# Shared channel rows of an mLSTM mixer computed as fp32 products in the two column halves of TensorE, results written to freed tiles, and a new task order

## Chip, cores and metric

One core of a Trainium2 chip. The metric is the device time in microseconds (us) of one execution, taken as the median of the runs. TensorE's two clock levels are 1.2 and 2.4 GHz; a granted clock of 1.00 in a row is 2.4 GHz, 0.50 is 1.2 GHz.

## The reference, cut to what matters

```python
for t in range(S):                      # S = 768, B = 4, H = 8, D = 40
    ...                                 # gates with a running maximum
    C = f_stab[:, :, None, None] * C + i_stab[:, :, None, None] * np.einsum('bhd,bhe->bhde', vt, kt)
    n = f_stab[:, :, None] * n + i_stab[:, :, None] * kt
    ...
    y[:, :, t] = o * h_tilde / denom
# x: y as (B, S, 320)
theta = x @ w_theta
zr = x * cos(theta); zi = x * sin(theta)
u = x + einsum('ts,bsd->btd', w_tok_r, zr) + einsum('ts,bsd->btd', w_tok_i, zi)
return u + maximum(u @ w_ch, 0.0)       # the channel product
```

All inputs are float32 in value; the weights of the mixer come to the chip as 64-bit words and are rounded there.

## The kernel before, in words

The kernel has three parts. The attention works in 24 units (6 chunks of 128 tokens by 4 batches): small fp32 products of 64-wide tiles (score L442, state L463, inter L482, intra L491). The mixer works in 12 pieces (a chunk by a pair of batches): five transposes (L538), the angle product (L554, L560), sine and cosine, and then five token products (L605, `mix`) of 12 matmuls each, whose result VectorE adds into `acc` (L630). `acc` holds u transposed: 10 tiles of 128 channel rows by 768 tokens, five for each pair of batches. Tile 2 of each five is shared: its upper 64 rows are the last 64 channels of the pair's first batch, its lower 64 rows the first 64 of the second batch.

The last part is the channel product, `channel()`. Each number that TensorE is to multiply with nearly full precision is split into a rounded high part and the rest (type fp32r, `_hi` and `_lo` tasks, and `uhi`, `ulo` at L669 and L670 for `acc`), and a product is made of three matmuls: high by high, low by high, high by low (`prods`, L680). Tiles 0, 1, 3 and 4 need two full blocks of 128 rows (L688) and one half block of 64 rows, which two tiles do at once in the two row halves of the array (L698). The shared tile 2 needs five full blocks, since its two batches' weights stand beside zeros in one 128-column operand: 5 blocks by 3 matmuls by 2 halves of the tokens are 30 matmuls for each pair of batches, at L688. VectorE adds the clipped result to `acc` in place (`relu`, L713), and SyncE sends the rows out (`out`, L715). The weights lie in two tiles of the pool `w`, with zeros between them (L641).

All work is a list of tasks; `ORDER`, a table written out by hand, gives the order of the tasks and each one's engine (T TensorE, V VectorE, A ScalarE, G GpSimd, D a DMA on SyncE's queue). Every engine runs its instructions in that order. `FILL` puts dummy matmuls of `ones` (L247) ahead of some TensorE tasks. Tiles come from small pools in the order of the tasks: four PSUM tiles `two`, three `tok`, three `z`, three `w`, two `raw`. A task that takes a buffer waits until the last user of that buffer is done.

Names used below: `tok4` is the load of the keys and values of attention unit 4 (L422), `w10` a block of token weights (L373), `st4` the state product of unit 4 (L463), `mix01` the token product of chunk 0, row tile 1, and `zl` the low part of a rotated mixer tile (L592).

Of the kernel before, what the change touches and what calls it, by code (L numbers as in the profile page):

```python
# [17 lines left out]
DM = H * D  # L18
# [15 lines left out]
WCOLS = 1792  # L34
# [6 lines left out]
4G 5T 6T 7T 8T 0D 14V 284V 85V 1D 21A 18A 12G 3G 30G 11V 13V 15D 43D 16D 55D 25V 27V 19V 28V 81V 29V 104D 47D 26V 44A  # L41
31V 82V 2D 32V 35A 83V 38V 37V 33A 17A 123D 39T 24A 56A 84V 280V 103D 34V 36V 42A 100A 99A 40A 282V 23V 86V 48A 109A
283V 102V 285V 101A 281V 49V 98A 41A 20A 110T 50V 90A 105T 22A 107T 57V 111V 51V 106A 128A 58V 52A 286V 108V 122D 59V
124T 125A 126T 53A 91V 127V 129T 212T 192D 130V 60A 292G 265G 61V 213A 74D 197A 131T 67D 132T 211D 54V 133V 139G 87V
134V 92V 135V 88A 75A 261G 62V 136V 291V 137V 112T 114V 113T 140V 138G 66A 193T 64A 63A 120G 93G 115V 116V 194A 117V
118V 121V 119V 198T 216A 76V 89V 94T 141T 77V 95A 97A 142A 143V 68A 96A 69V 78V 293T 263A 144A 65A 145T 70V 388D 191D
146T 296A 294A 295A 79A 147A 158T 71V 159T 195T 148V 160A 161V 199V 196V 72A 149A 162A 150A 200T 80G 297D 210D 45D
201T 163A 208G 202V 217T 214T 73V 151A 218A 203V 152V 219T 165V 204V 155V 166A 264V 273D 368D 167G 215V 369D 299D 221V
153A 220T 205V 209V 266D 222V 164A 154G 262A 168V 301T 223V 156V 169V 157V 179T 170V 298A 46A 224V 206V 302A 300D 320D
225V 207V 274A 305G 175T 180T 176T 325G 226V 229T 227V 228V 178A 232A 230A 275V 276V 181V 177V 327G 182A 171T 231V  # L50
172T 277V 173V 307G 303T 306T 304V 308V 376G 278A 267A 233T 234T 279G 374G 309T 235A 174V 321T 311V 236V 440D 310T
322A 319D 237A 326T 312V 313A 238A 268V 187T 314V 315V 317V 318V 316G 328V 188T 189V 183T 239A 323T 190A 329T 240V
243V 324V 184T 241A 287A 375T 331V 337G 242V 338V 244A 377V 330T 186A 185V 332V 245G 441A 378T 389D 386G 289A 333A
370T 380V 334V 269V 288V 387V 335V 252T 336G 253V 254V 371A 436A 438A 249T 390T 339T 270V 396G 391A 340A 251V 250V
456D 342V 341V 442V 255T 372T 373V 256V 343T 457D 611D 366D 437A 271A 367A 593A 344T 257A 462G 464G 394G 443V 395T
435A 345A 272V 379T 246T 397V 346V 381V 347A 444V 290V 349A 247V 398T 400V 348A 382V 392T 393V 258T 353V 439G 406G
350V 458T 248A 407V 260V 259V 463T 447D 354A 399T 465V 383V 546D 401V 478T 351A 459A 460T 352V 479A 402A 384V 403V
385V 525D 404V 477D 466T 355G 405G 445A 448A 468V 461V 356T 474G 449V 357V 408T 409A 358T 410V 412T 413T 450V 475V
411V 446G 359V 482G 533G 553G 454D 476D 455A 414A 467T 469V 415V 470A 594A 471V 595V 480T 483T 621G 484G 416A 418A
472V 417A 604D 523D 485V 481V 362T 473G 486T 363V 488V 494G 487T 547T 489V 495V 490A 422G 491V 423A 419V 420A 548A  # L60
360T 527T 364T 605A 750A 528A 424V 421V 492V 451V 365V 614D 425T 493G 452A 427T 606V 496T 607V 361V 426V 608V 453G
429T 526D 613D 545D 597D 524A 497A 598A 592A 619A 609A 531G 596G 753G 551G 498V 500T 501T 502A 428V 430V 529T 532T
599V 499V 610G 549T 530V 503V 431T 534V 504A 535T 505A 550V 600V 432V 506A 552T 543G 554V 536T 544V 537V 538V 555T
557V 507G 510V 508A 563V 433T 511A 615T 509V 911D 512G 564V 556T 434V 912A 617T 558V 634D 620T 601V 513T 616A 539A
540V 559A 560V 612A 602A 561V 541V 622V 562G 542G 514V 517T 618V 565T 633D 518V 566A 567V 568V 515T 623T 839D 683D
680D 688G 603G 569T 681A 639A 710G 570T 516V 625V 641V 571A 751A 631G 913V 632V 914V 572V 573V 575A 640T 624T 626V
642V 519T 574A 754D 643T 637T 520V 645V 682D 579V 635T 690G 651G 521T 652V 636A 580V 684T 576V 704T 638V 577A 685A
703D 522V 644T 689T 581G 686T 768D 702D 771D 705A 752A 627A 578V 628V 646V 749A 755A 647A 629V 691V 648V 586T 687V
692T 630G 649V 650G 708G 700G 587V 693T 653T 694V 654A 695V 756V 696V 701V 582T 772T 655V 773A 657T 658T 659A 656V
697V 583V 757V 706T 758V 660V 709T 661A 588T 698V 707V 711V 776G 712T 778G 699G 720G 589V 770D 663A 714V 713T 774T  # L70
721V 791D 662A 667V 777T 779V 715V 775V 759A 668A 590T 716A 717V 718V 664G 719G 584T 780T 790D 840D 669V 591V 585V
# [18 lines left out]
1112T 1113T 1114T 1140T 1117V 1125D 1141V 1143T 1115V 1116D 1118D 1142D 1144V 1145D  # L90
"""
FILL = """
39:6 107:2 110:6 113:3 124:2 126:2 200:1 201:1 214:2 217:2 219:2
"""


# [62 lines left out]
def mlstm_mixer(ctx: ExitStack, tc: tile.TileContext, gates, qk, tok, og, wtok, wth, wch, table_d, out):  # L159
# [472 lines left out]

    def channel():
        wc = [Tile(w_k, F32R), Tile(w_k, F32R)]
        wcv = lambda a: wc[a].t
        up = {}

        def zeros(e):
# [27 lines left out]
        for pr in range(2):  # L666
# [6 lines left out]
            if pr == 0:  # L673
                for jj in range(5):
                    pm[jj, 1] = pm[jj, 0]
# [157 lines left out]
```

## Time and profile before

| what | value |
|---|---|
| median of 3 runs | 296.83 us (296.46 to 298.31) |
| the profiled execution, its own time | 298.13 us |
| its span, first to last instruction | 296.3 us |
| mean granted TensorE clock | 0.987 |

The profile is of one execution, and durations are read from it; 1.8 us of its time lie outside the span. PE is TensorE's matmuls, PEld its weight loads, DVE VectorE, ACT ScalarE, POOL GpSimd, SP SyncE. The ends of matmuls are modelled, so that a pace is read from one start to the next, or from a piece of the chain of waits, and not from the mean of one.

### The profile page before, as it was taken

The numbers are of one execution on the slowest core, as the hardware profiler recorded it, in microseconds if no ns is written. First come the engines' busy times: TensorE is split into PE (matmuls) and PEld (weight loads), VectorE is DVE, ScalarE is ACT, GpSimd is POOL, SyncE is SP. The second block draws the span as 40 slices with busy tenths as digits, with TensorE's granted clock in tenths as the row PEclk, the third lists the DMA queues.
The fourth block names the chain that finished last, engine by engine and source line by source line (L and its number), as shares of the span: only waits on it lengthen the run. The fifth ranks groups of instructions, "written<-read, shape, count | busy, mean of one in ns | idle before, by whom it ended". The sixth has DMA issues, their size and how long they took to land.

```text
span 296.3 us, 10261 instructions
## 1 busy us (share of the span) xinstructions
PE 283.7 (96%) x4467; PEld 256.2 (86%) x4467; DVE 240.5 (81%) x449; ACT 180.8 (61%) x332; POOL 118.8 (40%) x125
## 2 busy tenths in 40 slices
PE   8598897999999999999999999999999999999995
PEld 3366677899899998999999999999999999999885
DVE  6869898699899998988998888888899697684342
ACT  6989998596876887858445493586377456120000
POOL 1003221635156474453517655333153529355000
PEclk9879999999999999999999999999999999999999
DMA  6967766545355551844417714525002000002334
GB/s 229 328 193 244 239 186 197 195 140 173 109 165 187 172 171 45 269 163 153 110 50 217 257 47 119 158 94 161 8 3 88 2 0 0 0 2 79 135 147 171
DMA packets 13484, 40.08 MB, mean 135 GB/s; under 512 B 1536, under 2 KB 3328, under 8 KB 13440
## 3 DMA queue, kind: packets, MB, share of 16 engines
q1 hardware_dynamic: 13440, 39.43, 41.7%
q8 instruction: 35, 0.57, 0.8%
q14 instruction: 9, 0.07, 0.1%
HBM read 35.49 MB, written 3.93 MB: 133 GB/s over the span
## 4 chain that ended last, share of the span: by engine, by line
PE 86%; DMA 5%; ACT 5%; DVE 1%; SPq 1%; issue 1%; POOL 0%; DVEq 0%
PE two L605 42%; PE two L688 10%; PE two L554 7%; PE two L442 4%; PE two L482 4%; PE two L491 4%; PE two L560 3%; PE two L463 3%; DMA tok<-in_tok 3%; PE two L430 3%; DMA raw<-in_wth 2%; PE two L538 2%; PE two L432 2%; ACT tok L451 2%; PE two L247 1%; PE two L698 1%
## 5 line engine op out<-in xcount | busy, mean ns | idle before, releaser
L605 PE MATMUL two<-w,z 128*128 128x384 f32 x720 | 135.5, 341 | 0.2 <-DVE hv L503 0.2
L605 PEld LDWEIGHTS two<-w,z 128*128 128x128 f32 x720 | 123.8, 188 | 1.8 <-issue 0.4
L630 DVE TENSOR_TENSOR acc<-two,acc 128x768 f32<-128x768 f32 x50 | 46.9, 951 | 12.3 <-PE two L605 11.9
L519 POOL TENSOR_TENSOR X<-hv,sg 128x320 f32<-128x320 f32 x18 | 16.1, 903 | 45.3 <-DVE sg L516 45.3
L688 PE MATMUL two<-u,w 128*128 128x384 f32 x156 | 28.7, 340 | 0.1
L688 PEld LDWEIGHTS two<-u,w 128*128 128x128 f32 x156 | 26.9, 188 | 1.4 <-issue 1.0
L368 POOL TENSOR_TENSOR w<-val,w 128x768 fp32r<-128x768 f32 (+2 forms) x11 | 20.1, 1832 | 12.9 <-ACT w L367 10.7
L473 POOL TENSOR_TENSOR C<-C,wane 128x164 f32<-128x164 f32 x34 | 17.2, 515 | 19.3 <-PE two L482 18.1
L554 PE MATMUL two<-wth,xs 128*128 128x320 f32 x144 | 23.7, 312 | 0.8 <-ACT wane L351 0.8
L713 DVE SCALAR_TENSOR_TENSOR acc<-two,acc 128x384 f32<-128x384 f32 (+1 forms) x15 | 9.7, 687 | 17.2 <-PE two L698 10.4
L554 PEld LDWEIGHTS two<-wth,xs 128*128 128x128 f32 x144 | 21.6, 188 | 1.4 <-ACT wane L351 1.0
L434 ACT ACTIVATE E<-two 128x512 f32<-128x512 f32 x24 | 14.1, 597 | 12.6 <-PE two L432 12.4
L564 ACT ACTIVATE r<-two 128x640 f32<-128x640 f32 (+1 forms) x13 | 8.6, 663 | 17.7 <-PE two L560 17.7
L445 DVE TENSOR_TENSOR E<-two,E 128x512 f32<-128x512 f32 x24 | 16.3, 682 | 3.2 <-PE two L442 2.1
L453 POOL TENSOR_TENSOR tok<-tok,fadeT 128x320 f32<-128x320 f32 x16 | 13.0, 815 | 12.2 <-DMA tok<-in_tok 12.1
L463 PE MATMUL two<-tok 64*40 64x41 f32 x768 | 13.2, 204 | 4.9 <-ACT tok L451 3.2
L592 POOL TENSOR_TENSOR z<-ab,z 128x640 fp32r<-128x640 f32 x8 | 14.2, 1779 | 8.5 <-ACT z L590 6.8
L670 POOL TENSOR_TENSOR u<-acc,u 128x768 fp32r<-128x768 f32 x7 | 14.4, 2068 | 8.0 <-DVE u L669 8.0
L463 PEld LDWEIGHTS two<-tok 64*40 64x40 f32 x768 | 10.6, 116 | 7.9 <-ACT tok L451 3.8
L482 PEld LDWEIGHTS two<-C,qk 40*64 40x64 f32 x768 | 13.8, 134 | 4.0 <-issue 2.1
L442 PEld LDWEIGHTS two<-qk 40*64 40x64 f32 x768 | 13.8, 138 | 4.1 <-issue 3.1
L442 PE MATMUL two<-qk 40*64 40x64 f32 x768 | 16.8, 227 | 0.0
(123 smaller groups left out, 534.2 us busy)
## 6 DMA issues: line engine op xcount, KB each, us to landing
qk<-in_qk SPq DMA_DIRECT2D x24, 448.0 KB, 4.9
raw<-in_wtok SPq DMA_DIRECT2D x12, 768.0 KB, 4.5
tok<-in_tok SPq DMA_DIRECT2D x24, 324.0 KB, 4.0
sg<-in_og SPq DMA_DIRECT2D x12, 320.0 KB, 4.2
out<-acc SPq DMA_DIRECT2D x5, 384.0 KB, 2.4
out<-acc SPq DMA_DIRECT2D x10, 192.0 KB, 2.3
raw<-in_wth SPq DMA_DIRECT2D x2, 480.0 KB, 7.0
raw<-in_wch SPq DMA_DIRECT2D x1, 640.0 KB, 3.8
```

The lines of the kernel that those rows point to most:

```text
L368: add(name + "_lo", "GV", lambda e: ENG[e].tensor_sub(lo(), o(), hi().bitcast(F32)), [val, *rest], step)
L442: nc.tensor.matmul(u.sc.t[half[x ^ f], f, k * L:(k + 1) * L], q4(1)[dims[f], k, s], q4(0)[dims[f], k, s], start=True, stop=True)
L445: add(f"wg{n}", "V", lambda e: nc.vector.tensor_mul(u.E.t, u.sc.t[:, :, :4 * L], u.E.t), [u.sc, u.E], n)
L463: nc.tensor.matmul(u.st.t[dims[f], x, k * E1:(k + 1) * E1], kt()[r, h], vt()[r, h], start=True, stop=True)
L473: add(f"cw{x}{n}", "GV", lambda e: ENG[e].tensor_mul(C[b][1 - x], C[b][x], f), (), n + 0.2)
L482: nc.tensor.matmul(u.it.t[half[x], f, k * E1:(k + 1) * E1], q4(0)[dims[f], k, s], C[b][x][dims[f], k], start=True, stop=True)
L519: add(f"X{n}", "VG", lambda e: ENG[e].tensor_mul(u.X.t[:, b % 2 * DM:(b % 2 + 1) * DM].rearrange("p (h d) -> p h d", d=D), u.hv.t[:, :, :D ...
L554: nc.tensor.matmul(th.t[:, b, :DM], xs.t[:, x, k], wt5[:, y, k], start=(i == l == 0), stop=False)
L605: nc.tensor.matmul(pm.t[:, t, :TH], Z[cc, pr].t[:, x, s, j * P:(j + 1) * P], wv(cc, y, s, t), start=(s == 1 and x == y == 0 and cc == mine ...
L630: add(f"ga{q}{j}", "V", lambda e, j=j, pm=pm, av=av: nc.vector.tensor_add(av, pm.t[:, :, :TH], av), [pm], n + 2.6 + 0.3 * j, swap="acc")
L670: add(f"ulo{pr}{k}", "VG", lambda e, pr=pr, k=k: ENG[e].tensor_sub(up[pr, k][:, 1], acc[:, 5 * pr + k], up[pr, k][:, 0].bitcast(F32)), (), ...
L688: nc.tensor.matmul(pv(jj, t), wcv(x)[:, col:col + P], up[pr, k][:, y, cols], start=(i == l == 0), stop=(jj == 2 and i == 4 and l == 2))
```

## The change

The shared tile 2 is no longer made of split operands. A small fp32 tile `wx` holds its weights whole: six blocks of 128 rows by 64 columns, three for each of the two batches (the two half blocks are filled up with zeros). The products are plain float32, with `acc` itself as the moving operand; the first batch's go to PSUM partitions 0 to 63 and the second's to 64 to 127, that is to the two column halves of the array, in turn (`shared`, L712 of the changed kernel). `uhi` and `ulo` stay, for the other tiles. Since `acc` must stay whole until then, `relu` writes into a tile of the pool `z` that the mixer has left, and `out` sends from there. The second pair of batches is no longer cut by halves of the tokens, but for its shared tile. The weights lie close together in `w`, so the four zero fills are gone; `wx` needs two smaller ones and seven copies. `_layout` sends the channel weights in the same form as the angle weights. `ORDER` is new for all tasks, and `FILL` has two dummy matmuls more.

```diff
-WCOLS = 1792
 ORDER = """
-4G 5T 6T 7T 8T 0D 14V 284V 85V 1D 21A 18A 12G 3G 30G 11V 13V 15D 43D 16D 55D 25V 27V 19V 28V 81V 29V 104D 47D 26V 44A
+4G 5T 6T 7T 8T 0D 30V 3V 1D 85G 11G 12G 14G 25V 43D 15D 27V 16D 55D 104D 2D 47D 17A 28V 123D 26V 103D 29V 122D 284G
...
 FILL = """
-39:6 107:2 110:6 113:3 124:2 126:2 200:1 201:1 214:2 217:2 219:2
+39:6 94:1 105:1 110:6 124:3 131:2 141:3 198:1 200:2 201:1 214:2 219:3
 """
...
+            up["wx"] = upool.tile([P, 6, L], F32, name="wx")
...
+        def zeros(e):
+            nc.scalar.activation(wx()[L:, 2], ident[L:, :L], AF.Copy, scale=0.0)
+            nc.scalar.activation(wx()[:L, 5], ident[:L, :L], AF.Copy, scale=0.0)
+
+        def whole0(e):
+            v = vals[0].t
+            COPY[e](wx()[:, 0:2], v[:, :2 * DM].rearrange("p (k n) -> p k n", k=2)[:, :, 4 * L:])
+            COPY[e](wx()[:L, 3], v[L:, 0:L])
+            COPY[e](wx()[L:, 3], v[:L, DM:DM + L])
+            COPY[e](wx()[:L, 4], v[L:, DM:DM + L])
...
-            fulls = {0: [(0, 0), (1, 704)], 1: [(0, P), (1, 704 + P)], 3: [(3, 384 + 64), (4, 1088 + 64)],
-                     4: [(3, 384 + 64 + P), (4, 1088 + 64 + P)], 2: [(0, 256), (1, 960), (2, 1664), (3, 320), (4, 1024)]}
...
+            def shared(t, pr=pr, pm=pm):
+                cols = slice(t * TH, (t + 1) * TH)
+                for i in range(3):
+                    for g in range(2):
+                        k = 2 if i == 2 else 3 * g + i
+                        nc.tensor.matmul(pm[2].t[L * g:L * g + L, t, :TH], wx()[:, 3 * g + i], acc[:, 5 * pr + k, cols],
+                                         start=(i == 0), stop=(i == 2))
+
+            def leave(jj, o, t0, t1, late, pr=pr, pm=pm):
+                ov = lambda: o.t.rearrange("p a s n -> p (a s n)")[:, (jj // 3) * S + t0 * TH:(jj // 3) * S + t1 * TH]
...
+                add("relu" + tag, "V", lambda e: nc.vector.scalar_tensor_tensor(
+                    ov().rearrange("p (h t) -> p h t", t=TH), pm[jj].t[:, t0:t1, :TH], 0.0, a, op0=ALU.max, op1=ALU.add),
+                    [pm[jj], o], late)
...
+            o = Tile(z_k)
+            for t in range(2):
+                add(f"chs{pr}{t}", "T", lambda e, t=t, shared=shared: shared(t), [pm[2]], base + 1.7 + 0.1 * t, half=True)
```

TensorE's queue where the token products end and the channel products begin, before (`two`: the PSUM tile written; `z`, `w`, `u`: mixer tile, weights, split u):

```order
L605 MATMUL two_65<-w_3222,z_3615 128x384 x12
L605 MATMUL two_68<-w_3222,z_3615 128x384 x12
L605 MATMUL two_66<-w_3222,z_3615 128x384 x12
L688 MATMUL two_68<-u_3649,w_3611 128x384
L688 MATMUL two_68<-u_3649,w_3612 128x384
```

And the same place in the changed kernel (L694 is L688 of before):

```order
L605 MATMUL two_65<-w_3189,z_3692 128x384 x12
L605 MATMUL two_68<-w_3189,z_3692 128x384 x12
L605 MATMUL two_67<-w_3189,z_3692 128x384 x12
L712 MATMUL two_66<-acc,wx 64x384 x12
L605 MATMUL two_68<-w_3189,z_3692 128x384 x12
L694 MATMUL two_67<-u_3584,w_3680 128x384
L694 MATMUL two_67<-u_3584,w_3681 128x384
```

The shared tile of the first pair of batches (12 fp32 products of 64 output rows) now stands ahead of the last token product; that of the second pair stands at the very end of the queue.

SyncE's queue some 40 us into the program, before (`qk`, `tok`, `sg`, `raw`: loads of queries and keys, keys and values, output gates, and token weights):

```order
L373 DMA raw_70<-in_wtok 128x768
L421 DMA qk_101<-in_qk 112x1024
L422 DMA tok_103<-in_tok 128x648
L421 DMA qk_100<-in_qk 112x1024
L373 DMA raw_69<-in_wtok 128x768
L422 DMA tok_105<-in_tok 128x648
```

And in the changed kernel:

```order
L373 DMA raw_70<-in_wtok 128x768
L421 DMA qk_102<-in_qk 112x1024
L409 DMA sg_108<-in_og 128x640
L422 DMA tok_105<-in_tok 128x648
L421 DMA qk_101<-in_qk 112x1024
L409 DMA sg_106<-in_og 128x640
L422 DMA tok_104<-in_tok 128x648
L373 DMA raw_69<-in_wtok 128x768
```

The last two rows before are `w10` and then `tok4`; in the changed kernel `tok4` stands ahead of `w10`, and it takes the buffer of unit 3 instead of unit 2's.

VectorE's queue at the same time, before (`hv`, `den`, `sg`: attention result, its divisor, the gate; `ab`: the rotated mixer values; `z`: their split halves, of which the second `zl` is the last that the token product's second operand needs):

```order
L505 TENSOR_TENSOR hv_112<-two_65,hv_112 128x328
L588 TENSOR_TENSOR ab_77<-ab_77,X_73 128x320
L511 TENSOR_SCALAR den_110<-hv_112 128x8
L590 CAST z_675<-ab_77 128x320 x2
L592 TENSOR_TENSOR z_675<-ab_77,z_675 128x320 x2
L514 RECIPROCAL den_110<-den_110 128x8
L516 SCALAR_TENSOR_TENSOR sg_108<-den_109,sg_108 128x320
L516 SCALAR_TENSOR_TENSOR sg_108<-den_110,sg_108 128x320
```

And in the changed kernel:

```order
L505 TENSOR_TENSOR hv_112<-two_66,hv_112 128x328
L592 TENSOR_TENSOR z_661<-ab_77,z_661 128x320
L511 TENSOR_SCALAR den_110<-hv_112 128x8
L588 TENSOR_TENSOR ab_77<-ab_77,X_73 128x320
L514 RECIPROCAL den_110<-den_110 128x8
L590 CAST z_661<-ab_77 128x320
L516 SCALAR_TENSOR_TENSOR sg_107<-den_110,sg_107 128x320
L516 SCALAR_TENSOR_TENSOR sg_107<-den_109,sg_107 128x320
L592 TENSOR_TENSOR z_661<-ab_77,z_661 128x320
```

The second `zl` has moved behind the two gate steps. On TensorE the two halves of `mix01` now stand together (12 matmuls in one row), so that the second operand is asked for after 6 matmuls instead of 12.

## Rows read from the trace of the kernel before

**Rows 1.** The page, part 1: busy us (share of span) xinstructions of each engine

```profile
PE 283.7 (96%) x4467; PEld 256.2 (86%) x4467; DVE 240.5 (81%) x449; ACT 180.8 (61%) x332; POOL 118.8 (40%) x125
```

**Rows 2.** Busy time by stage, three stretches

```profile
core 0: us, PE busy (x) PEld busy (x) DVE busy (x) ACT busy (x) POOL busy (x), PEclk, DMA share, GB/s
...
52.00:234.00 182.00, 181.56 (x3364) 169.76 (x3360) 161.90 (x296) 122.92 (x198) 86.64 (x93) 1.00 0.42 132
234.00:259.50 25.50, 25.50 (x147) 25.44 (x146) 18.15 (x24) 10.80 (x22) 13.70 (x8) 1.00 0.00 1
259.50:293.00 33.50, 33.42 (x204) 30.54 (x203) 16.27 (x21) 1.48 (x2) 8.60 (x4) 1.00 0.27 101
```

**Rows 3.** The chain that ended last, channel products: start us, us, what

```profile
259.49 8.34 PE two L688 x48
267.84 1.27 PE two L698 x11
...
270.21 8.62 PE two L688 x48
278.83 0.72 PE two L698 x6
...
281.53 2.30 PE two L688 x12
...
287.60 5.44 PE two L688 x30
...
293.06 0.56 DVE acc L713
```

**Rows 4.** PE timeline, fp32 products: start us, us, engine line op tiles xcount

```profile
28.98 0.66 PE L343 MATMUL two<-tab,z 128*64 128x32 f32 x16
29.46 0.64 PE L347 MATMUL two<-tab,w 128*64 128x32 f32 x16
...
60.51 0.69 PE L442 MATMUL two<-qk 40*64 40x64 f32 x32
61.02 0.63 PE L482 MATMUL two<-C,qk 40*64 40x41 f32 x32
```

**Rows 5.** Groups by line, kept apart by form: the score products

```profile
L442 PE MATMUL two<-qk 40*64 40x64 f32 x768 | 16.8, 227 | 0.0
```

**Rows 6.** The chain at 127 us: five fp32 transposes of 128 columns

```profile
127.05 0.55 PE two L538 x5
```

**Rows 7.** PE timeline, 42 to 52 us; in brackets idle time before, and releaser

```profile
42.29 4.34 PE L605 MATMUL two<-w,z 128*128 128x384 f32 x24
...
49.20 0.69 PE L442 MATMUL two<-qk 40*64 40x64 f32 x32
51.52 0.52 PE L463 MATMUL two<-tok 64*40 64x41 f32 x32 [1.63 <-POOL tok L453]
```

**Rows 8.** The chain at 41 us: SyncE's issue of `w10`, then `tok4`

```profile
41.52 1.18 SPq L373
...
42.74 7.93 DMA tok<-in_tok
...
50.74 0.73 POOL tok L453
```

**Rows 9.** DVE timeline, 41.8 to 45 us

```profile
41.82 0.49 DVE L505 TENSOR_TENSOR hv<-two,hv 128x328 f32<-128x328 f32 x1
42.23 0.48 DVE L588 TENSOR_TENSOR ab<-ab,X 128x320 f32<-128x320 f32 x1
...
42.70 0.56 DVE L590 CAST z<-ab 128x320 fp32r<-128x320 f32 x2
43.17 0.89 DVE L592 TENSOR_TENSOR z<-ab,z 128x320 fp32r<-128x320 f32 x2
...
44.09 0.84 DVE L516 SCALAR_TENSOR_TENSOR sg<-den,sg 128x320 f32<-128x320 f32 x2
```

More of the change, by code (lines that the diff above doesn't have):

```diff
@@ L368, in split @@
         add(name + "_lo", "GV", lambda e: ENG[e].tensor_sub(lo(), o(), hi().bitcast(F32)), [val, *rest], step)
+        return val
     def raw_load(name, src, step):
@@ L671, in channel, with product, product2 @@
                     up[pr, k][:, 1], acc[:, 5 * pr + k], up[pr, k][:, 0].bitcast(F32)), (), base + 0.3 * k, [opened])
[L672 to L684 removed]
+            pm = {jj: Tile(two) for jj in range(5)}
+            def product(jj, pr=pr, pm=pm):
+                g, col = side[jj]
+                for t in range(2):
                     cols = slice(t * TH, (t + 1) * TH)
[L686 removed]
+                    for i in range(2):
                         for l, (x, y) in enumerate(prods):
[L688 to L692 removed]
+                            nc.tensor.matmul(pm[jj].t[:, t, :TH], wcv(x)[:, 3 * g + i, col:col + P], up[pr, 3 * g + i][:, y, cols],
+                                             start=(i == l == 0), stop=False)
+            def product2(j0, pr=pr, pm=pm):
+                for t in range(2):
                     cols = slice(t * TH, (t + 1) * TH)
@@ L695, in product2 @@
                         for jj in (j0, j0 + 3):
-                            f, col = halfs[jj]
-                            rows = slice(64 * f, 64 * f + 64)
-                            nc.tensor.matmul(pv(jj, t), wcv(x)[rows, col:col + P], up[pr, 2][rows, y, cols],
+                            g, col = side[jj]
+                            rows = slice(L * g, L * g + L)
+                            nc.tensor.matmul(pm[jj].t[:, t, :TH], wcv(x)[rows, 2, col:col + P], up[pr, 2][rows, y, cols],
@@ new lines, in shared @@
+            def shared(t, pr=pr, pm=pm):
[7 more added lines that the diff above has]
+                ov = lambda: o.t.rearrange("p a s n -> p (a s n)")[:, (jj // 3) * S + t0 * TH:(jj // 3) * S + t1 * TH]
+                cols = slice(t0 * TH, t1 * TH)
+                tag = f"{pr}{jj}" + ("" if t1 - t0 == 2 else str(t0))
+                a = acc[:, 5 * pr + jj, cols].rearrange("p (h t) -> p h t", t=TH)
+                add("relu" + tag, "V", lambda e: nc.vector.scalar_tensor_tensor(
+                    ov().rearrange("p (h t) -> p h t", t=TH), pm[jj].t[:, t0:t1, :TH], 0.0, a, op0=ALU.max, op1=ALU.add),
+                    [pm[jj], o], late)
+                load("out" + tag, lambda: dma(
+                    out[(5 * pr + jj) * P:(5 * pr + jj + 1) * P, cols], ov()), [o], late + 0.1)
@@ new lines, in channel @@
+            for j0 in range(2):
+                for jj in (j0, j0 + 3):
+                    add(f"ch{pr}{jj}", "T", lambda e, jj=jj, product=product: product(jj), [pm[jj], *wc], base + 1.0 + 0.1 * jj)
+                add(f"chh{pr}{j0}", "T", lambda e, j0=j0, product2=product2: product2(j0), [pm[j0], pm[j0 + 3], *wc], base + 1.5,
+                    half=True)
+                o = Tile(z_k)
+                for jj in (j0, j0 + 3):
+                    leave(jj, o, 0, 2, base + 1.6)
+            o = Tile(z_k)
@@ L718, in mlstm_mixer @@
+            for t in range(2):
+                add(f"chs{pr}{t}", "T", lambda e, t=t, shared=shared: shared(t), [pm[2]], base + 1.7 + 0.1 * t, half=True)
+                if pr == 1:
+                    leave(2, o, t, t + 1, base + 1.8 + 0.1 * t)
+            if pr == 0:
+                leave(2, o, 0, 2, base + 1.8)
     for i in range(1, len(CUTS) - 1):
```

177 lines of the change are left out of this document (73 added, 104 removed).

## The prediction

> **What bounds the kernel now.** I read the page's first part, then the busy time by stage, then the chain of waits, and last the timelines of the two places where the change can act. TensorE is busy for 96% of the span, VectorE for 81% [rows 1]; "busy" is flattering for matmuls, whose ends are modelled, so the stages decide. Between 52 and 234 us TensorE's matmuls cover 181.56 of 182.00 us, between 234 and 259.5 all of 25.50, and in the channel products 33.42 of 33.50 [rows 2]. The reader is to see that from 52 us on nothing but fewer or shorter matmuls can shorten the program, and that a new order there has 0.5 us to gain at most and any amount to lose. Only before 52 us does TensorE wait: 1.63 us at 51.52, for the keys of unit 4 [rows 7]. The chain names what was behind that wait: SyncE spends 1.18 us on the issue of `w10`, and `tok4` behind it takes 7.93 us to land [rows 8].
>
> **The shared tile, removed.** Five blocks by three split products by two halves of the tokens are 30 matmuls a pair of batches, 60 in all. Two runs of 48 like matmuls took 8.34 and 8.62 us [rows 3], 0.177 us each. 60 x 0.177 = 10.6 us go. They stand on the path: the last 30 are the piece of 5.44 us that ends the program's matmuls [rows 3].
>
> **The shared tile, added.** Per pair of batches 12 fp32 products of 64 output columns by 384 tokens. The trace shows that an fp32 product is two instructions: the score loop writes 16 products a unit, 384 over 24 units, and the profile has 768 [rows 5]. So 24 instructions a pair of batches, 48 in all. If those of the two column halves run side by side, that is 24 passes in a row.
>
> Do they? The score products use all four quarters of the array, with four different moving operands: 32 of them in 0.51 us, from 60.51 to the next group's start [rows 4], that is 64 ns for four. The two column halves with 128 rows appear in the end-of-chunk transposition of the gates: 16 instructions in 0.48 us [rows 4], 60 ns for a pair, but with only 32 columns. Four quarters of 64 columns in the time in which two halves handle 32 says that the time is a floor there, not the columns; so the quarters run together, and I take the halves to do so as well.
>
> How long is a pass of 384 columns? The trace has no fp32 matmul so wide. From below: no faster than an fp32r matmul of 384 columns, 0.177. From above: the score's 64 ns for 64 columns, scaled by six, 0.38. The nearest row is the transpose: fp32, one pass, 128 columns, five in 0.55 us [rows 6], 0.11 each; three times that is 0.33, which I take. 24 x 0.33 = 7.9 us come (4.2 to 9.2). Balance of the shared tile: 10.6 - 7.9 = 2.7 us saved (1.4 to 6.4).
>
> The Trainium skill has a rule that would make more of it: Perfetto Trace Analysis, section Engine Utilization, gives the array's output rate as halved for the fp32 low-high form. Read as two passes of which each runs at full rate, that would be 0.16 to 0.18 us a pass and 4.2 us in all; by the transposes' row a pass is slower than that, but with 128 weight columns to load per transpose that row can also be a floor. It is a rival below. For the column halves the skill speaks for the change (TensorEngine Tiling, Key Properties: tiles work independently and can run matmuls in parallel); by it the pair is one pass, and without it the sum would be that of the last rival. The rows agree for quarters of the array; for halves with 384 columns no row here shows it.
>
> **Changes of the array's form.** A block of three pairs in row halves takes 0.72 us where 3 x 0.177 is 0.53, and the twelve full matmuls behind it 2.30 where 2.12 is due [rows 3]: 0.19 us on the way in and as much on the way out. Before, there are five such blocks in the channel products, ten changes. Now the second pair isn't cut by token halves: into and out of the first shared tile, two blocks with a full one between and behind, then a block that goes straight into the last shared tile: eight. 2 x 0.19 = 0.4 us saved (0 to 0.6, as a change from row to column halves is not in the trace).
>
> **What hides the rest.** `relu` has the same size and engine, and writes elsewhere; at the end it is still one of 384 columns behind the last product (0.56 at 293.06) [rows 3], and the last DMA has its size of before, so the tail of 3.3 us stays. `uhi` and `ulo` stay, all twenty. The zero fills and the copies into `wx` are ScalarE's, which is busy for 10.80 of 25.50 us there and 1.48 of 33.50 later [rows 2]: nothing, unless they come late for the first shared tile, and then as much as they are late. That tile needs no `ulo`, but all five sums of the first pair; its place, eleven token products (11 x 2.1 us) into the stage at about 257 us, is 8 us behind the last of those products, which covers them.
>
> VectorE is where the new order presses. It gets two `zl`, both halves of a weight split, six copies of 64 rows and three `ulo` in the last token stage: from the sum of `mix92` at about 238.3 to the last sum of the stage I count 33 instructions in the queue, and at the stage's mean of 18.15 / 24 = 0.76 us [rows 2] that is 25 us, against 27 us until TensorE needs the PSUM tile behind it. Covered, with 2 us to spare; if the cover goes, TensorE waits for PSUM. I take 0 (0 to 3 lost).
>
> **The start.** With `tok4` ahead of `w10` the wait of 1.63 goes. What is late next? `mix01` asks for its second operand after 6 matmuls, at 42.29 + 6 x 0.177 = 43.35. On VectorE that operand's last step, `zl`, now stands behind the gates: from 42.23 (`hv` done) half of 0.89, then 0.1 for the divisor, 0.48, 0.1, half of 0.56, 0.84 and half of 0.89 again [rows 9], 2.7 us in all: 44.9. (The 0.1s are estimates, from what the rows leave between their neighbours.) TensorE waits 1.55 us there; from 43.35 on it has 6.54 us of work until the score at 49.20 has ended [rows 7], so the state product starts at 44.9 + 6.54 = 51.4, and before at 51.52. `tok4` and 0.73 us of POOL must be there by then, which leaves it about 8.5 us from 41.5, when its buffer comes free. One wait takes the other's place: 0.1 us saved (1.6 saved, if the operand comes in time; 1.5 lost, if the start itself is late by as much as this wait and nothing behind it gives way). Behind that point the order on TensorE is nearly that of before, with as many changes of form, and I take nothing for it (0.4 saved to 2 lost).
>
> **Sum.** 2.7 + 0.4 + 0.1 = 3.2 us. Against the profiled execution: 298.13 - 3.2 = 294.9. That execution is 1.3 us above the median of the runs, 296.83; against the median, 293.6 us, which is 1.1% less. A measurement of this kernel tells about 1%, 3 us, from no change, so the forecast lies just beyond it.
>
> **Rivals.**
> 1. A pass streams at fp32r's rate. For it: the transposes' 0.11 us may be a floor of weight loading, as the 60 and 64 ns of small products are. Against: the nearest fp32 row by width stays the transposes, and nothing in the rows shows an fp32 pass of more than 128 columns at that rate. 24 x 0.177 = 4.2 instead of 7.9: 3.7 us less, 289.9. Chance 0.12.
> 2. VectorE becomes the bound of the last token stage, or some other wait of the new order takes back most of the gain. For it: 25 of 27 us, and casts at fp32 width that stretch whenever POOL works beside them. Against: POOL has less to do there now. Price 2 to 3 us: 296.1. Chance 0.2.
> 3. The start's wait goes without another: 1.5 us more, 292.1. For it: rows 8; against: the VectorE queue as worked out. Chance 0.05.
> 4. The other side: the column halves run one after the other. Place: the four shared tiles' halves, 4 us in the middle and 4 us at the very end, nothing beside them. Then 48 passes of 0.33 are 15.8 us, 5.2 more than the 60 matmuls removed; less 0.5 for forms and start, 4.7 us slower: 301.5. It decides from a pass of 10.6 / 48 = 0.22 us on. Against it: four quarters in 64 ns [rows 4]. Chance 0.05.
>
> **How the numbers follow.** The forecast holds 0.58, with 292.2 to 295.3 as its own range; beyond 1% (293.9) lies some 0.6 of it. Faster by over 1%: 0.36 of the forecast, with rivals 1 and 3, 0.53. Within 1%: 0.22 of the forecast and most of rival 2, 0.38. Slower: 0.09, from rival 4 and the worst of rival 2. The range reaches from rival 1 to a little beyond rival 2, 289.9 to 297.0.
>
> **What would show it.** Right: L712 as 48 records, two at a time, passes 0.33 us apart, each of the four pieces about 2 us; the last shared tile takes 4.0 us in all where the piece of before took 5.44; no idle time of PE over 0.3 us from 234 us on; at 43 us PE waits some 1.5 us for DVE's `z`, and no longer for `tok`. Wrong: L712 starts spread singly over 8 us a pair of batches (rival 4), pieces of 1 us (rival 1), PE waiting for `acc` sums or `u` of DVE or POOL behind 240 us (rival 2), or new idle time of PE between 52 and 234 us, of which I foresee none.

## The result, and the profile after

| | before | changed |
|---|---|---|
| median of 20 runs | 298.15 us | 299.35 us |
| lowest | 295.46 us | 294.14 us |
| profiled execution: span, mean granted clock | 296.3 us, 0.987 | 298.6 us, 0.966 |

Ratio of the times 0.991, 95% interval [0.988, 0.994]: 0.9% faster, against 1.1% forecast. The ratio leaves out executions that lie over 1.5% above the fastest of their kernel; of the changed kernel these are 12 of 20 (298.8 to 301.2 us, and the profiled one is among them), so that by the medians of all runs the changed kernel is 0.4% slower. What sets these executions apart is part of the story: a second fall of TensorE's clock, which the new order invites.

The page after, part 1's busy row and the clock's row of part 2 (40 slices of 7.5 us, tenths of 2.4 GHz):

```profile
PE 285.3 (96%) x4451; PEld 253.3 (85%) x4457; DVE 241.8 (81%) x450; ACT 195.4 (65%) x405; POOL 109.3 (37%) x115
...
PEclk9869758999999999999999999999999999999999
```

Two dips of the clock stand there, in slices 2 and 3 (0.50 from 12.9 to 19.7 us) and again in slices 5 to 7 (33.4 to 47.0 us). Before had the first alone (12.3 to 19.2 us). Busy time by stage (columns as in [rows 2]):

```profile
42.00:52.00 10.00, 9.57 (x201) 7.71 (x197) 7.00 (x21) 7.84 (x15) 2.61 (x4) 0.75 0.63 185
52.00:234.00 182.00, 181.60 (x3417) 169.73 (x3416) 161.61 (x303) 141.83 (x277) 82.09 (x83) 1.00 0.44 138
234.00:259.50 25.50, 25.50 (x153) 25.11 (x152) 23.82 (x33) 10.18 (x21) 8.11 (x5) 1.00 0.00 1
```

From 52 us on TensorE's matmuls cover as much as before [rows 2], and the granted clock is 1.00. The stages come some 5 us later than before, so that the last row, cut as in [rows 2], isn't quite the last token stage: that begins at 239.00. In the 25.50 us from there VectorE is busy for 23.65 with 34 instructions, TensorE for all of them, so that VectorE delays nobody. The chain of waits at the end (start us, us, what):

```profile
239.00 23.16 PE two L605 x132
262.15 4.02 PE two L712 x24
266.18 2.29 PE two L605 x12
268.47 4.19 PE two L694 x24
272.66 1.25 PE two L704 x10
273.91 8.53 PE two L694 x48
282.44 2.30 PE two L704 x24
284.74 4.43 PE two L694 x24
289.17 1.25 PE two L704 x12
290.42 4.04 PE two L712 x24
...
294.49 0.56 DVE z L720
```

L712 is the shared tile: 24 records, two at a time, in 4.02 and 4.04 us, where the split tile took 5.44 [rows 3]. There is no hole between the pieces.

Most of what was lost lies at the start. ScalarE's and TensorE's timelines there, first of the kernel before:

```profile
27.82 1.86 ACT L451 ACTIVATE tok<-tok,fadeT 128x40 f32<-128x40 f32 x8
...
31.36 1.14 PE L554 MATMUL two<-wth,xs 128*128 128x320 f32 x6 [0.84 <-ACT wane L351]
```

And of the changed kernel:

```profile
28.88 1.86 ACT L451 ACTIVATE tok<-tok,fadeT 128x40 f32<-128x40 f32 x8 [1.64 <-DMA tok<-in_tok]
...
31.58 0.69 ACT L540 CAST xs<-two 128x640 fp32r<-128x640 f32 x1
...
33.05 0.20 ACT L350 ACTIVATE leaveT<-two 128x32 f32<-128x32 f32 x1
```

```profile
29.41 0.77 PE L538 MATMUL two<-ident,X 128*128 128x128 f32 x5 [0.63 <-DVE X L519]
...
33.30 1.93 PE L554 MATMUL two<-wth,xs 128*128 128x320 f32 x6 [1.66 <-ACT leaveT L350]
...
56.52 0.49 PE L463 MATMUL two<-tok 64*40 64x41 f32 x32
```

ScalarE stands 1.64 us at the scaling of `tok3` (task `fade3`, L451). Behind it on its queue are the rounding of the first transposed piece (L540) and, with two steps on weights between, the copies out of the table product (L350), the last of which ends TensorE's wait. TensorE waits 0.63 us ahead of the transposes at 29.41 and 1.66 us ahead of the theta product (L554) at 33.30; before, the scaling had no wait and that product started at 31.36. Its six matmuls take 1.93 us here, where the same six take 1.15 in e1 below: from 33.37 to 47.02 us the granted clock is 0.50. The state product of unit 4 starts at 56.52 instead of 51.52 [rows 7].

Four marks divide the time: the start of that state product, of the last theta product, of the last `relu`, and the span's end (starts from the timelines; us).

| | state product | to last theta | to last `relu` | to the end | span |
|---|---|---|---|---|---|
| before | 51.52 | 182.31 | 59.23 | 3.29 | 296.35 |
| changed | 56.52 | 182.17 | 56.27 | 3.59 | 298.55 |
| e1, changed again | 53.64 | 182.07 | 56.26 | 3.59 | 295.56 |
| e2, old start | 51.92 | 182.22 | 56.27 | 3.60 | 294.01 |
| e4, start filled | 49.91 | 182.57 | 56.28 | 3.59 | 292.35 |
| e5, own tile | 50.87 | 182.24 | 55.79 | 3.53 | 292.43 |
| e8, both edits | 50.06 | 182.26 | 55.80 | 3.55 | 291.67 |

The second column is the long middle: 182.1 to 182.6 in all, no gain and no loss. The third is 2.96 us shorter with the change, the fourth 0.30 longer. Everything else is the first column. It also holds how an execution gets going: the first state product starts at 12.3 to 14.1 us, and the clock's first fall lasts 3.4 us (e1, e4), 6.8 (before, changed, e2, e5, e8) or 10.2 (e12). So the start is better read from the theta product to unit 4's state product: 20.16 us before, 23.22 in the changed kernel, 21.76 in e1, 17.94 in e4, 19.61 in e2, 18.41 in e5, 18.33 in e8.

### The profile page after: what moved, and what is told of

Read it like the earlier page. It is cut to its first block, busy times and chain, and to the rows that moved or that the text cites. A ratio compares the mean times of both kernels' runs of the same rounds, so it can differ in the third digit from the quotient of the medians.

```text
span 298.6 us, 10296 instructions
## 1 busy us (share of the span) xinstructions
PE 285.3 (96%) x4451; PEld 253.3 (85%) x4457; DVE 241.8 (81%) x450; ACT 195.4 (65%) x405; POOL 109.3 (37%) x115
## 4 chain that ended last, share of the span: by engine, by line
PE 88%; DMA 4%; ACT 3%; DVE 2%; issue 1%; SPq 1%; DVEq 0%; ACTq 0%
PE two L605 43%; PE two L554 8%; PE two L694 6%; PE two L442 4%; PE two L491 4%; PE two L482 4%; PE two L560 3%; PE two L712 3%; PE two L430 3%; PE two L463 3%; DMA raw<-in_wth 2%; PE two L538 2%; PE two L432 2%; DMA tok<-in_tok 2%; PE two L704 2%; PE two L246 1%
## 5 line engine op out<-in xcount | busy, mean ns | idle before, releaser
L367 POOL TENSOR_TENSOR w<-val,w 128x768 fp32r<-128x768 f32 (+1 forms) x12 | 22.9, 1911 | 14.5 <-ACT w L366 9.0
L451 ACT ACTIVATE tok<-tok,fadeT 128x40 f32<-128x40 f32 x112 | 26.0, 318 | 1.6 <-DMA tok<-in_tok 1.6
L554 PE MATMUL two<-wth,xs 128*128 128x320 f32 x144 | 25.2, 325 | 1.7 <-ACT leaveT L350 1.7
L554 PEld LDWEIGHTS two<-wth,xs 128*128 128x128 f32 x144 | 22.9, 199 | 2.3 <-ACT leaveT L350 1.8
L473 POOL TENSOR_TENSOR C<-C,wane 128x164 f32<-128x164 f32 x31 | 15.5, 505 | 24.0 <-PE two L482 20.0
L720 DVE SCALAR_TENSOR_TENSOR z<-two,acc 128x768 f32<-128x768 f32 (+1 forms) x11 | 9.2, 879 | 14.3 <-PE two L704 12.1
L684 POOL TENSOR_TENSOR u<-acc,u 128x768 fp32r<-128x768 f32 x5 | 9.9, 1994 | 25.7 <-ACT u L683 22.5
L694 PE MATMUL two<-u,w 128*128 128x384 f32 x96 | 17.4, 338 | 0.0
L482 PE MATMUL two<-C,qk 40*64 40x41 f32 x768 | 16.9, 232 | 0.5 <-issue 0.4
L694 PEld LDWEIGHTS two<-u,w 128*128 128x128 f32 x96 | 16.6, 188 | 0.6 <-DVE z L720 0.3
L491 PE MATMUL two<-tok,E 64*64 64x41 f32 x768 | 16.3, 231 | 0.6 <-DVE E L445 0.3
```

Of the source, the lines that this page charges most:

```text
L367: add(name + "_lo", "GV", lambda e: ENG[e].tensor_sub(lo(), o(), hi().bitcast(F32)), [val, *rest], step)
L451: nc.scalar.mul(kt()[:, h], kt()[:, h], f[:, h:h + 1])
L473: add(f"cw{x}{n}", "GV", lambda e: ENG[e].tensor_mul(C[b][1 - x], C[b][x], f), (), n + 0.2)
L482: nc.tensor.matmul(u.it.t[half[x], f, k * E1:(k + 1) * E1], q4(0)[dims[f], k, s], C[b][x][dims[f], k], start=True, stop=True)
L491: nc.tensor.matmul(u.ph.t[half[x], f, k * E1:(k + 1) * E1], u.E.t[r, f, k * L:(k + 1) * L], vt()[r, 4 * f + k], start=True, stop=True)
L554: nc.tensor.matmul(th.t[:, b, :DM], xs.t[:, x, k], wt5[:, y, k], start=(i == l == 0), stop=False)
```

## The experiments

The theory: the shared tile's products give some 3.4 us wherever they stand, the start's new order opens idle time on TensorE, and the clock's second fall follows from that. Its rivals: the gain hangs on the order, the start is late by waits alone, or the column halves don't overlap.

**e1. The changed kernel again**, no edit. 

> The changed kernel once more, to see an execution in which TensorE's clock stays at 2.4 GHz behind 20 us. Theory (the last stage gives 3.4 us, the new order of the start takes back some of it, and in the execution shown the second fall of the clock, 33.4 to 47.0 us, takes the rest): where that fall is absent the state product of unit 4 starts near 52.2 instead of 56.5, the stretch from the end of thh11 to the z of the last piece is again 56 us (59.6 before), and the time is 294 to 296, about 2.7 under the kernel before on the same chip. Rival (the start is late by its waits alone, the clock has no part): the state product stays near 56 and the time near 299 in every execution.

Measured: 297.34 us, the median of 12 (294.14 to 300.42), 0.994 [0.990, 0.998] of before. The clock fell in the profiled execution too, but later and for less long, 34.0 to 44.3 us; theta product at 31.88, state product at 53.64. ScalarE's wait was there as well:

```profile
27.46 1.86 ACT L451 ACTIVATE tok<-tok,fadeT 128x40 f32<-128x40 f32 x8 [1.18 <-DMA tok<-in_tok]
...
31.88 1.15 PE L554 MATMUL two<-wth,xs 128*128 128x320 f32 x6 [1.58 <-ACT leaveT L350]
```

So the 52.2 for a start without the fall stays untried here. The last stage repeats to 0.01 us, and the span is 3.0 us shorter. The state product is 2.9 us earlier: 1.4 of this lie ahead of the theta product, where the first fall was shorter too, and 1.5 behind it, where the second was 3.4 us shorter. The executions at 294.1 beside those at 300 speak against waits that make every execution late.

**e2. Old start, changed rest.**

```diff
 ORDER = """
-4G 5T 6T 7T 8T 0D 30V 3V 1D 85G 11G 12G 14G 25V 43D 15D 27V 16D 55D 104D 2D 47D 17A 28V 123D 26V 103D 29V 122D 284G
+4G 5T 6T 7T 8T 0D 14V 284V 85V 1D 21A 18A 12G 3G 30G 11V 13V 15D 43D 16D 55D 25V 27V 19V 28V 81V 29V 104D 47D 26V 44A
...
```

> The changed code with the order and the filling matmuls of the kernel before up to unit 4's state product, and the changed order behind it. Theory: the start costs what it cost before (state product near 51.5, clock at 2.4 GHz from 20 us on), the two shared tiles still take 4.0 us each, so the time is 3.0 to 3.6 under before, some 0.7 under the changed kernel where that is undisturbed. Rival (the gain of the last stage needs the new start, as the loads and the places of the first stage set when the later ones come free): new idle time of TensorE between 52 and 234 us, and the time within 1 us of before.

Measured: 295.80 us (293.46 to 296.81 in 12 runs), 0.993 [0.989, 0.996] of before. No second fall of the clock, the wait for `tok4` back (1.08 us on TensorE, state product at 51.92), and the middle as full as ever, 181.55 of 182.00 us. The gain doesn't need the new start. It is 2.2 us by the ratio, below the 3.0 to 3.6 expected; part of what is missing is in the tail, which from the first of the two last `relu`s to the end is 0.8 us longer than before and e5's subject.

**e3. Old order throughout**, with the changed code: the shared tile's products at the places of the split ones, the results' order of before. 

> The changed code in the order of the kernel before throughout: the shared tiles as fp32 products in the column halves, at the places where the split products of the same tiles stood. Theory (the gain is that of the products themselves, not of the order): two shared tiles of 4.0 us against 5.4 for one with splits, start as before, 2.4 to 3.4 under before. Rival (the new order is what makes the gain, as the freed mixer tiles or the leaving of the results need it): the shared tiles take 4.0 us too, but TensorE waits between the channel products, and the time is within 1 us of before.

Measured: 300.80 us (299.99 to 301.85), 1.010 [1.006, 1.015] of before: 1.0% slower. VectorE's and TensorE's timelines at the end:

```profile
290.49 0.56 DVE L720 SCALAR_TENSOR_TENSOR z<-two,acc 128x384 f32<-128x384 f32 x1 [3.47 <-DMA out<-z]
...
291.10 4.11 PE L712 MATMUL two<-acc,wx 128*64 128x384 f32 x12 [4.72 <-DVE z L720]
```

The results now leave through three tiles of pool `z`. In the old order the last tile's first half finds none free and waits for an output to land; the second half's products wait for that `relu`, 4.72 us, and the clock falls in the meantime, so that twelve records take 4.11 us instead of 2.0. So the theory fell in part: the products are as fast in any order (4.09 for the first pair's 24), but the freed tiles make the order of the channel products a condition of the gain.

**e4. Idle time filled**: more dummy matmuls ahead of the transposes and of the last turn.

```diff
-39:6 94:1 105:1 110:6 124:3 131:2 141:3 198:1 200:2 201:1 214:2 219:3
+39:6 94:1 105:1 110:6 124:3 131:2 141:7 198:1 200:2 201:1 214:2 219:3 293:7
```

> The changed kernel with more filling matmuls in TensorE's two idle stretches ahead of the theta product (3 to 7 ahead of the transposes at 28 us, 0 to 7 ahead of the last turn at 31 us); they compute nothing that is read. Theory (the idle of 2.3 us in all there lets the clock fall at 33 us in some executions): the clock stays at 2.4 GHz behind 20 us in all of them, state product near 52.2, every time near that of the best executions of the changed kernel, 294 to 296. Rival (the fall has another cause than the idle time): the granted clock still falls at 33 us and times near 299 to 300 remain; a second rival (the filling delays the turn): clock kept, but thf0l starts later than 33.3 by up to 2 us, and so does the end.

Measured: 295.05 us in the median (293.70 to 298.75), 0.992 [0.989, 0.996] of before. One execution of 12 took over 298.5 us, of the changed kernel 5 of 12 in e1, on the same chip, and 17 of 32 with the first measurement. In the profiled one the clock stays at 1.00 from 17.2 us to the end of the matmuls, the theta product starts at 31.97 and the state product at 49.91, with no wait for `tok4`:

```profile
31.97 1.15 PE L554 MATMUL two<-wth,xs 128*128 128x320 f32 x6
...
42.50 4.33 PE L605 MATMUL two<-w,z 128*128 128x384 f32 x24
...
44.77 0.48 DVE L592 TENSOR_TENSOR z<-ab,z 128x320 fp32r<-128x320 f32 x1
...
49.91 0.49 PE L463 MATMUL two<-tok 64*40 64x41 f32 x32
```

This execution and e1's are alike up to there: a first fall of 3.4 us, a wait of ScalarE for `tok3` of 1.25 and 1.18 us, the theta product at 31.97 and 31.88. But where e1's TensorE is idle for 1.58 us, it has dummy matmuls here, and from the theta product to the state product it takes 17.94 instead of 21.76 us. So in this pair filled gaps keep the clock up where open ones let it fall. Not in every execution, though: half of the executions still have a mean granted clock of 0.975 to 0.986, against 0.991 to 0.999 of the others.

**e5. A PSUM tile of its own** for the second half of the last shared tile, on e2.

```diff
+                if pr == t == 1:
+                    pm[2] = Tile(two)
```

> The kernel of e2 (changed code, old start) in which the second half of the last shared tile has a PSUM tile of its own and the first half's relu and output stand ahead of it. Theory (the tail after the last matmul grew from 3.3 to 4.1 us, since the first half's relu waits for both halves' matmuls in one tile, and its output then stands ahead of the last one on SyncE's queue): the first half's relu runs beside the last twelve passes, the tail is 3.3 us again, 0.7 to 0.8 us under e2 on the same chip. Rival (the tail is longer because the rows now leave from a tile of the pool z): the tail stays at 4.1 us and nothing is gained.

Measured: 294.74 us (before 297.25 on the same chip), 0.992 [0.990, 0.995]. VectorE's end in the changed kernel and in e5:

```profile
294.49 1.02 DVE L720 SCALAR_TENSOR_TENSOR z<-two,acc 128x384 f32<-128x384 f32 x2 [2.20 <-PE two L712]
```

```profile
286.97 0.56 DVE L721 SCALAR_TENSOR_TENSOR z<-two,acc 128x384 f32<-128x384 f32 x1 [0.27 <-PE two L712]
288.90 0.56 DVE L721 SCALAR_TENSOR_TENSOR z<-two,acc 128x384 f32<-128x384 f32 x1 [1.38 <-PE two L712]
```

In the changed kernel both `relu`s of half a tile stand behind all 24 records; in e5 the first runs beside the second half's passes. From the last theta product to the last `relu` it is 55.79 instead of 56.27 us: 0.48 gained of the 0.7 to 0.8 expected. The last 0.24 stay behind the `relu`, and weren't followed further. Against e2, on another chip, the two ratios can't tell 0.5 us apart.

**e6. Column halves one after the other**, on e2.

```diff
-                for i in range(3):
-                    for g in range(2):
+                for g in range(2):
+                    for i in range(3):
```

> The kernel of e2 with the shared tile's loops exchanged: the three products of one column half first, then those of the other, the same products in all. Theory of the prediction (products of the two column halves run side by side when they stand in turn): now only neighbours in the queue can overlap, a pair of batches takes 6.5 to 7.7 us instead of 4.02, and the time is 5 to 7.5 us above e2. Rival (TensorE passes 48 instructions in 4.02 us whatever column half they go to, that is 0.16 us each): 4.02 us again and no difference to e2.

Measured: 297.31 us, 1.000 [0.998, 1.003] of before: 0.7% worse than e2 on another chip, some 2 us; 1.4 us by the chain:

```profile
256.93 4.72 PE two L712 x24
...
285.87 4.73 PE two L712 x24
```

0.70 us more for each pair of batches: the loop order matters, and TensorE doesn't pass the 24 records of a pair of batches one after another whatever their place, as the rival had it (its 48 are those of both pairs). But it is far from the 6.5 to 7.7 us of serial halves. The starts of the last 24 records, beside e4's, tell why:

```
e4: 284.144 284.151 | 284.518 284.524 | 284.840 284.847 | ...
e6: 285.796 | 286.169 | 286.492 286.498 | 286.814 286.871 | 287.137 287.194 | ... | 289.774 | 290.096
```

Only the first two and the last two passes are alone. I read this as TensorE letting a pass of the idle half go beside one of the busy half, though several of the latter stand ahead of it in the queue.

**e7. `tok4` ahead of `w10`**, on e2: task 300, the load of `tok4`, ahead of 266, that of `w10`.

```diff
-153A 220T 205V 209V 266D 222V 164A 154G 262A 168V 301T 223V 156V 169V 157V 179T 170V 298A 46A 224V 206V 302A 300D 320D
+153A 220T 205V 209V 300D 266D 222V 164A 154G 262A 168V 301T 223V 156V 169V 157V 179T 170V 298A 46A 224V 206V 302A 320D
```

> The kernel of e2 with one load moved: tok4 ahead of w10 on SyncE's queue, as in the changed kernel, while VectorE keeps its old order. Theory of the prediction (the wait for tok4 comes from the issue of w10 ahead of it): the state product of unit 4 waits no longer and starts 1.2 to 1.6 us earlier, near 50.4; 1.0 to 1.5 us under e2. Rival (tok4 is late since its buffer comes free late, and w10 ahead of it costs it nothing, or w10 behind it is late for the token product): the wait stays or turns up at the first product with w10, within 0.4 us of e2.

Measured: 293.73 us (292.88 to 295.26), 0.988 [0.985, 0.991]. The wait is gone, and nothing takes its place: 1.4 us by the ratios against e2, on another chip. The state product in e2, e7 and e5:

```profile
51.92 0.52 PE L463 MATMUL two<-tok 64*40 64x41 f32 x32 [1.08 <-POOL tok L453]
```

```profile
50.99 0.49 PE L463 MATMUL two<-tok 64*40 64x41 f32 x32
```

```profile
50.87 0.52 PE L463 MATMUL two<-tok 64*40 64x41 f32 x32
```

But e5 has `w10` ahead of `tok4` too, as have e3 and e6, and none of these three has the wait in its profiled execution: the load landed earlier there (in e3 issued at 43.70 and used by POOL at 49.16, before at 42.74 and 50.74). From the theta product to the state product they take 18.32 to 18.52 us, e7 18.35. So a trace without the wait doesn't show by itself what the edit is worth; the times of e8 against e5 and of e9 against before do.

**e8. Both edits**, e5's and e7's. 

> Both of these edits together, the version that should beat both kernels: e2 less 1.0 to 1.5 for tok4 and less 0.7 for the tail, 293 to 294 in the median where e2 gives 295.8, with the clock at 2.4 GHz behind 20 us as in e2. Rival (the start's edit is worth nothing): e5's time.

Measured: 293.37 us (292.57 to 295.03), 0.987 [0.984, 0.990] of before, in the middle of the range expected; 1.4 us under e5's 294.74, on the same chip and with `tok4` moved as the only difference. The timeline has no wait ahead of the state product, and the clock stays up:

```profile
49.55 0.69 PE L442 MATMUL two<-qk 40*64 40x64 f32 x32
50.06 0.49 PE L463 MATMUL two<-tok 64*40 64x41 f32 x32
```

**e9. The kernel before with `tok4` ahead of `w10`**, nothing else. 

> The kernel before, unchanged but for one load: tok4 ahead of w10 on SyncE's queue. Theory (the start's wait for tok4 and the shared tile are independent terms, and the first can be had without the change): state product of unit 4 about 1.3 us earlier, 1.0 to 1.6 us under before; e7 less e2 was about 2. Rival (the step pays only with the changed kernel's other edits, or w10 is late instead): within 0.5 us of before.

Measured: 296.49 us (before 298.06 on that chip), 0.996 [0.994, 0.999]: 1.1 us, the lower end of what was expected. State product at 49.85, 18.33 us behind the theta product where before had 20.16. So this part of e8's gain could be had without the change.

**e10. `fade3` later**, on the changed kernel: task 216 on ScalarE behind the rounding of the first transposed piece.

```diff
-193T 211D 112T 89V 135V 291V 136V 197A 62V 63A 194A 140V 75A 114V 92G 113T 191D 64A 94T 137V 115V 216A 96A 66A 120G
-116V 45D 210D 320D 388D 138G 121V 198T 117V 118V 119V 76V 141T 13V 293T 77V 142A 68A 143V 95A 97A 264A 144A 65A 145T
+193T 211D 112T 89V 135V 291V 136V 197A 62V 63A 194A 140V 75A 114V 92G 113T 191D 64A 94T 137V 115V 96A 66A 120G 116V
+45D 210D 320D 388D 138G 121V 198T 117V 118V 119V 76V 141T 13V 293T 77V 142A 68A 143V 95A 97A 264A 144A 216A 65A 145T
```

> The changed kernel with one step of ScalarE moved: the scaling of tok3 (eight small instructions, which wait 1.2 to 1.6 us for that load) behind the rounding of the first transposed piece instead of ahead of it. Theory (TensorE's idle time before the theta product, and with it the fall of the granted clock at 33 us, comes from ScalarE standing at tok3 with that rounding behind it): xs is rounded some 1.3 us earlier, thf0l starts near 30.6 instead of 31.9 to 33.3, TensorE's idle time there falls under 1 us, the clock falls at 33 us in few executions or none, and the median is 293 to 294.5 where the changed kernel's is 297 to 299. Rival (the idle time comes from VectorE's X or from the table product ahead of thf0l): thf0l stays at 31.9 or later and the times stay spread up to 300.

Measured: 293.21 to 301.75 us, median 295.45 of six. Three executions at 293.2 to 293.4 are better than any of the changed kernel, the others took 297.5 to 301.8. In the profiled one, of the latter kind, the theta product starts at 30.89, as expected, but further on TensorE waits again:

```profile
30.89 1.15 PE L554 MATMUL two<-wth,xs 128*128 128x320 f32 x6 [0.29 <-ACT leaveT L350]
...
34.20 0.71 PE L554 MATMUL two<-wth,xs 128*128 128x320 f32 x3 [0.89 <-ACT wth L387]
...
36.11 1.13 PE L442 MATMUL two<-qk 40*64 40x64 f32 x32 [0.57 <-ACT wane L350]
```

What was moved on ScalarE has only pushed other steps behind it: a split of theta weights, the table copies. The granted clock is 0.50 from 35.5 to 49.1 us. The first step of the theory held, the second only in part: the idle time ahead of theta went, but other idle time came, and the clock is lower again in half of the executions. Three of 6 executions here, and 3 of 7 of e11, have a mean granted clock of 0.99 or more, of the changed kernel 5 of 32; these are too few to tell by how much the fall became rarer.

**e11. The same with e5's tile.** 

> The same, and the second half of the last shared tile in a PSUM tile of its own as in e5: 0.4 to 0.5 us under e10. Rival (the chain's end moves to another output): no difference to e10.

Measured: 293.09 to 299.96 us, median 296.03 of seven; its three best, 293.1 to 293.5, stand beside e10's 293.2 to 293.4, so that the 0.4 to 0.5 expected can't be told from nothing here.

**e12. e8 with `fade3` later still**, behind the theta weights' split too. 

> The kernel of e8 with the scaling of tok3 on ScalarE moved as in e10, but behind the last split of the theta weights too, which TensorE waited 0.89 us for in e10. Theory (ScalarE's queue ahead of the rounding of the first transposed piece sets the start of thf0l in the old start as well, 1.9 us of scaling between them): thf0l about 0.9 us earlier, no new idle time of TensorE over 0.5 us between 28 and 40 us, the clock at 2.4 GHz from 20 us on, and 0.5 to 0.9 us under e8: 292.4 to 293 in the median. Rival (the gain is lost at the next wait, or the idle time that it opens lets the clock fall, as in e10): thf0l earlier but the state product of unit 4 not, or times spread up to 298.

Measured: 297.33 us (294.01 to 301.93), 0.998 [0.995, 1.001] of before: 4 us worse than e8's median, on another chip. The theory's first step held in part: TensorE's wait ahead of theta is 0.33 instead of e8's 0.82 us, and theta starts 4.30 us behind unit 3's state product instead of 4.80. (Counted from the first state product nothing is seen of it, 19.12 and 19.13 us, but the clock's first fall lasted 10.2 us here and 6.8 in e8.) The rest fell, as TensorE waited behind theta:

```profile
37.10 0.70 PE L442 MATMUL two<-qk 40*64 40x64 f32 x32 [0.44 <-ACT wane L350]
38.68 0.38 PE L246 MATMUL two<-ones 128*128 128x512 bf16 x1 [0.88 <-DVE r L580]
```

The clock fell from 40.1 to 43.5 us. Without the scaling ScalarE is idle for 1.00 us ahead of the rounding, so that over half of its 1.86 us had cost nothing in the old place; the move put it in front of steps that TensorE needs. e8 stays the best version, by 1.3% under before, and with no execution above 295.03.

## Why the prediction was right, and where its steps failed

The forecast was 293.6 us (1.1% less than before); the ratio says 0.9% less, within the range. The main term, the shared tile, held in mechanism and size. But two steps failed, in opposite directions, and a loss at the start had no term at all.

- *The shared tile.* Right. A pair of batches is 24 records in 4.02 us, 12 passes of two side by side; 2 x (5.44 - 4.02) = 2.84 us saved, or 2.56 if the 60 split matmuls are priced at 0.177 us each as in the sum, 2.7 forecast. The estimate of 0.33 us for a pass, from transposes of 128 columns [rows 6], measured 0.322 (starts above). Rival 1, the fp32r rate, is out: 0.322 is 1.8 times 0.177, and the halving of the Trainium skill's Perfetto Trace Analysis, section Engine Utilization, as that rival read it, isn't what this pass shows. Rival 4 is out: pairs start 7 ns apart, as the Trainium skill's TensorEngine Tiling (Array Packing), section Key Properties, would have it.
- *Changes of form.* 0.4 forecast. From the last theta product to the first of the two last `relu`s it is 55.80 us (56.27 less the 0.47 between the two), 3.43 less than before; without the shared tile's 2.56 to 2.84 that leaves 0.59 to 0.87, at the upper bound given or above it. No run separates the changes of form from what else became different there.
- *The tail.* The step failed: "at the end it is still one of 384 columns behind the last product", "so the tail of 3.3 us stays". It was two `relu`s, and 4.06 us from the first of them to the end: 0.77 lost. e5 got 0.48 of it back. In all the last stage gave 2.66 us, where the sum had 3.1.
- *VectorE in the last token stage.* Right: from the sum at 243.40 to the end of the last at 266.52 it is 31 instructions in 23.1 us, where 33 in 25 us were forecast, and no wait of TensorE. The first half of rival 2 has no place there.
- *The start, `zl`.* The step failed: "`mix01` asks for its second operand after 6 matmuls". It reads columns 128 to 255 of the operand, which are the first batch's alone; the second batch's `zl` is first asked for by `mix02`, some 20 matmuls in. In e4 that is at 42.50 + 20 x 0.177 = 46.0, and the `zl` is there at 44.77 + 0.48 = 45.25. So the wait of 1.63 went with nothing in its place, rival 3's mechanism and the bound "1.6 saved, if the operand comes in time": from the theta product to the state product e4 takes 17.94 us, and before 20.16, or 18.53 without its wait. e9 takes 18.33 with the one load moved. But the 1.63 are a price of that execution: e3, e5 and e6 keep the old order of the loads, and their profiled executions don't wait.
- *The start, upstream.* What the sum had no term for: "`tok4`" was the only load that I followed. `tok3` isn't issued late (at 22.5 us in e1 and 23.8 in the profiled execution, 23.3 before), but ScalarE's new order comes to its scaling before it has landed. That idle time is small, but in most executions more time at 1.2 GHz follows: 24 of 32 have a mean granted clock under 0.98, of the kernel before's 85 in e1 to e12 one. Where the second fall is seen, it costs more than the whole last stage gives: from the theta product to the state product 5.28 us more than in e4 in the profiled execution, 3.82 in e1. This is the other half of rival 2, "some other wait of the new order takes back most of the gain", at a place where the prediction didn't look and, where the fall is long, above its price of 2 to 3 us.

That forecast and result agree to 0.2% is in part luck: the start saves more than the 0.1 us forecast where the clock stays (1.6 us at the state product of e4, half a microsecond of it from an earlier first product), the tail takes back 0.8, and the executions in the ratio have the clock's falls in varying length. Over all executions there is no gain to agree with: the medians are 299.35 and 298.15 us, and in e1 297.34 and 297.50.

Filling the gaps makes the fall rarer (e4, 1 of 12 against 5 of 12 on its chip); that new gaps elsewhere bring it back fits e10 and e12, but isn't isolated there. Why the same kernel falls in one execution and not in the next isn't settled, nor how much idle time it takes: from 20 to 33 us TensorE is idle for 2.1 us before, with no second fall, for 2.9 in e1 and for 1.5 in e10, both with one.

## What to carry to other kernels

A few fp32 products that use both column halves of the array can beat a threefold split where the split's operand is half zeros: here 12 passes of 0.32 us, two products side by side in each, for 30 of 0.18. But a new order is as good as its worst gap: ask for every engine, not only for the one load that is late now, which instruction comes before its data, and what stands behind it. Near the end of a program, count the tiles through which results leave, and give pieces that are to leave one by one a PSUM tile each.

## What the runs showed of the hardware that I had not expected

- Waits of TensorE of 1.66 and 1.58 us ahead of the theta product were followed by 13.7 and 10.2 us at 1.2 GHz (changed kernel, e1), although TensorE was at work for nearly all of that time (13.01 of 13.70 us, and all of 10.30). Against e4, where dummy matmuls filled the wait, this cost 5.28 and 3.82 us by the state product: two to three times the wait.
- An fp32 pass follows the clock: 0.322 us at 2.4 GHz, and 0.640 with the granted clock at 0.50 (from pair to pair of e3's last twelve records).
- TensorE overlaps products of the two column halves even where they don't stand in turn, as I read e6's pairs: three products of one half ahead of three of the other cost 0.70 us in 4.
- The same load takes a different time in each execution: `tok4` 7.93 us from issue to landing before [rows 8], but in e3, issued at 43.70, it was in use at 49.16. A wait for a load seen in one execution need not be there in the next.
